# Batch 1's q and k loaded as fp32 on SyncE's queue and cast on GpSimd, in a kernel with a written-out order

## The chip, the cores and the metric

The kernel runs on one core of a Trainium2 chip. A core has TensorE (PE in the rows: matmuls, and PEld for loading weights), VectorE (DVE), ScalarE (ACT), GpSimd (POOL) and SyncE (SP), which here only issues transfers. Matmuls write PSUM; the other engines move and compute between PSUM and SBUF, GpSimd in SBUF alone. DMA engines move data between HBM and SBUF; a transfer is issued by an instruction on an engine's queue. The metric is the device time of one execution in microseconds. Each engine does its instructions in the order in which they were written, and waits for those of other engines by semaphores.

## The reference

Attention with a forget gate over 8 batches, 8 heads, 576 positions and 64 dimensions, then a bilinear feed-forward layer over its 4608 tokens:

```python
scores = scale * np.matmul(q, k.transpose(0, 1, 3, 2))
log_f = np.log(np.clip(f, 0.0001, 1.0))
cum = np.cumsum(log_f, axis=-1)
decay = cum[:, :, :, None] - cum[:, :, None, :]
scores = np.where(causal, -1000000000.0, scores + decay)
scores = scores - np.max(scores, axis=-1, keepdims=True)
attn = np.exp(scores)
attn = attn / (np.sum(attn, axis=-1, keepdims=True) + 1e-09)
attn_out = np.matmul(attn, v)
...
x = attn_out.transpose(0, 2, 1, 3).reshape(B * S, H * D)
a = x @ w_a            # 512 x 1536
b = x @ w_b            # 512 x 1536
out = a * b @ w_out    # 1536 x 512
```

Inputs and output are fp32; the kernel multiplies in fp16.

## The kernel before

**Work units.** A pair is two heads of one batch; there are 32 pairs, numbered t = 4 x batch + pair. The 576 queries of a pair are five blocks (0 to 3 of 128, 4 of 64), each against the keys up to it. For a pair the steps are: scores on TensorE (`qk_group`, line 449, tile sc, PSUM); maximum on VectorE (batch 0, line 546) or decay and maximum in one pass into the tile S (line 572, later batches); exponential on ScalarE with row sums (lines 599 and 603); reciprocal on VectorE (611 and 613); normalisation on GpSimd (line 621, into PA for blocks 0 to 2 and PB for 3 and 4); transposition of the probabilities, by DMA from SyncE (635) or on TensorE (641, batch 0 and blocks 0 to 2 of batch 1) with an eviction; product with v on TensorE (663 and 679, tile pv); eviction to xT, the feed-forward input. For batch 0 the decay is added by TensorE, from the cumulative sum in the tile crow; for batch 1 it is spread over partitions by a TensorE step (514, the "spread step") and an eviction; from batch 2 on by a DMA (525).

**Feed-forward.** Tokens go in chunks of 256, 256, 256, 384, six times 512, and 384. A chunk has 12 pairs of steps psa and psb (line 950), a copy of a by ScalarE (255), a product on VectorE (961), and then the output matmuls pso (970).

**q and k.** A batch's q, and its k, come in two halves (`load_qk`). A half is four heads; the eight batches and two tensors make 32 halves. Two forms exist. In the first, a DMA on GpSimd's queue casts to fp16 on the way (line 286), and TensorE transposes 64 x 64 blocks in four quadrants (`pe_transpose`, line 307, 36 matmuls); q's scale 1/8 is applied when the transposed tile is evicted (257 and 253). In the second, a DMA on SyncE's queue brings fp32 (291) into a buffer of the ring n32, GpSimd casts it to fp16 and scales q (257 for q, 259 for k), and TensorE transposes 128 columns at a time in two row halves (18 matmuls); the eviction then has no scale (255 and 259). The ring n32 has three buffers, which v uses too. `EARLY` names the batches of the first form, and also those with other settings (three score steps for a pair, separate parts of PA); it is batches 0 and 1.

**The order.** Every step is an `Op` with an engine (or several to choose from). `ORDER` lists the 2460 numbers of the ops in the order in which their instructions are written, which sets each engine's order; `CHOICE` has a letter for each op with a choice of engine (D VectorE, A ScalarE, P GpSimd). Dependencies of the ops themselves set nothing at run time; the semaphores follow from tiles and their buffers. At the start stand the load and logarithm of f, its cumulative sum (195 and 200), the identity (masks.py), constants and paddings on GpSimd, and 24 wake steps (78), each two matmuls on the identity, on TensorE. The weights come by casting DMAs on GpSimd's queue (424).

## Time and profile before

| what | value |
|---|---|
| time, median of 3 runs | 409.13 us (408.86 to 409.19) |
| the profiled execution | 408.86 us |
| its span | 407.1 us |
| TensorE busy | 396.3 us (97%) |
| VectorE busy | 301.6 us (74%) |
| ScalarE busy | 282.5 us (69%) |
| GpSimd busy | 262.3 us (64%) |
| granted TensorE clock, mean | 0.998 |
| DMA queue of SyncE and ScalarE (q1), share of 16 engines | 72.2% |
| DMA queue of GpSimd (q0), share of 16 engines | 11.2% |

A row of the order of time gives start, duration, engine, line, operation, tiles and shapes, a count of like instructions in a row, and in brackets the idle time before it and what ended that. A matmul's duration includes its way through the array, so two starts tell the pace, not two durations. A row of groups gives a count, busy time and mean duration in ns.

### The profile page before, as it was taken

To read this page: it belongs to the slowest core of one execution; us is meant where nothing else is said; L and a number is where in the kernel's file an instruction comes from. 1 tells how busy PE (TensorE), PEld (TensorE's weight loads), DVE (VectorE), ACT (ScalarE), POOL (GpSimd) and SP (SyncE) were. 2 spreads that over 40 slices of the span, in tenths; PEclk is the share of its full clock that TensorE was granted. 3 is DMA by queue.
4 is the path that set the end of the run, shared out by engine and by line. 5 is a ranking of instruction groups with operands and counts; after the bars stand their busy time and mean duration, and the time that the engine had idled before them with its cause. 6 is when DMAs were issued, how large, how long until landed. Compare 5 with 4: busy or idle time off the path is not lost.

```text
span 407.1 us, 11321 instructions
## 1 busy us (share of the span) xinstructions
PE 396.3 (97%) x4028; PEld 213.4 (52%) x4028; DVE 301.6 (74%) x1007; ACT 282.5 (69%) x796; POOL 262.3 (64%) x490
## 2 busy tenths in 40 slices
PE   6899999999999999999999999999999999999996
PEld 2457675766755554444445454444444444444552
DVE  3887998997979778878868789688888874442241
ACT  3898988888977778778787877568785873231230
POOL 8997697778876786886787767849666555000000
PEclk9999999999999999999999999999999999999999
DMA  8999998999999999999999999999895768100102
GB/s 126 205 190 199 152 217 194 203 271 233 249 196 221 320 229 208 276 199 229 204 275 253 278 237 166 317 250 206 205 189 159 143 116 179 52 2 32 74 0 77
DMA packets 147176, 76.65 MB, mean 188 GB/s; under 512 B 124336, under 2 KB 129200, under 8 KB 147120
## 3 DMA queue, kind: packets, MB, share of 16 engines
q1 hardware_dynamic: 141040, 68.73, 72.2%
q0 software_dynamic: 5936, 7.08, 11.2%
q8 instruction: 31, 0.51, 0.5%
q14 instruction: 25, 0.20, 0.2%
q10 hardware_dynamic: 144, 0.13, 0.1%
HBM read 52.05 MB, written 9.58 MB: 151 GB/s over the span
## 4 chain that ended last, share of the span: by engine, by line
PE 74%; DVE 3%; issue 1%; ACT 0%; DVEq 0%
PE pso L970 22%; PE psb L950 20%; PE psa L950 20%; PE sc L449 6%; PE pv L663 4%; PE psT L307 1%; DVE S L572 1%; DVE ht L961 1%; PE sc L679 1%; PE pv L679 0%; PE psP L641 0%; DVE qT L259 0%; DVE st L613 0%; DVE half L259 0%; DVE st L572 0%
## 5 line engine op out<-in xcount | busy, mean ns | idle before, releaser
L572 DVE CUSTOM_DVE_ANT_0 S<-sc,spread 64x576 f32<-64x576 f32 (+4 forms) x232 | 126.3, 562 | 16.3 <-PE sc L449 6.3
L950 PE MATMUL psb<-xT,wb 128*128 128x512 f16 (+2 forms) x528 | 115.3, 341 | 0.0
L950 PE MATMUL psa<-xT,wa 128*128 128x512 f16 (+2 forms) x528 | 115.2, 341 | 0.0
L255 ACT CAST a<-psa 128x512 f16<-128x512 f32 (+2 forms) x132 | 66.4, 503 | 56.6 <-PE psa L950 47.2
L621 POOL TENSOR_SCALAR PA<-PA,st 128x256 f16<-128x256 f16 (+2 forms) x192 | 89.1, 476 | 23.8 <-DVE st L613 19.3
L961 DVE TENSOR_TENSOR ht<-psb,a 128x512 f16<-128x512 f32 (+2 forms) x132 | 77.4, 590 | 35.7 <-PE psb L950 30.5
L970 PE MATMUL pso<-wout,ht 128*128 128x512 f16 x432 | 99.8, 380 | 0.0
L603 ACT ACTIVATE PA<-S,st 128x256 f16<-128x256 f32 (+2 forms) x168 | 84.6, 505 | 10.9 <-DVE st L572 10.6
L621 POOL TENSOR_SCALAR PB<-PB,st 128x512 f16<-128x512 f16 (+1 forms) x96 | 67.4, 709 | 33.3 <-DVE st L613 14.3
L950 PEld LDWEIGHTS <-wa 128*128 128x128 f16 x528 | 49.1, 98 | 40.5 <-issue 2.1
L950 PEld LDWEIGHTS <-wb 128*128 128x128 f16 x528 | 49.1, 98 | 40.2 <-issue 2.0
L970 PEld LDWEIGHTS <-ht 128*128 128x128 f16 x432 | 39.8, 98 | 45.2 <-issue 0.9
L603 ACT ACTIVATE PB<-S,st 128x512 f16<-128x512 f32 x56 | 40.1, 717 | 8.0 <-DVE st L572 7.8
L449 PE MATMUL sc<-kT,qT 64*128 64x128 f16 (+4 forms) x384 | 34.4, 266 | 2.4 <-ACT PA L603 0.9
L603 ACT ACTIVATION_READ_ACCUMULATOR PA<-S,st 128x1 f32 x168 | 32.1, 191 | 0.0
L259 DVE CAST xT<-pv 128x512 f16<-128x512 f32 (+1 forms) x40 | 23.1, 578 | 5.0 <-PE pv L663 4.8
L449 PEld LDWEIGHTS <-qT 64*128 64x128 f16 (+1 forms) x384 | 13.5, 95 | 23.8 <-issue 16.2
L613 DVE RECIPROCAL st<-st 128x2 f32<-128x2 f32 x128 | 18.1, 157 | 10.2 <-ACT PB L603 5.9
L599 ACT ACTIVATE PB<-S,st 128x576 f16<-128x576 f32 x28 | 21.7, 776 | 5.5 <-POOL PA L621 1.9
L259 DVE COPY osb<-pso 128x512 f32<-128x512 f32 x17 | 11.7, 688 | 17.9 <-PE pso L970 17.8
L255 ACT COPY osb<-pso 128x512 f32<-128x512 f32 x18 | 10.4, 579 | 20.6 <-PE pso L970 14.4
L663 PEld LDWEIGHTS <-nv 128*64 128x64 f16 x640 | 19.1, 109 | 10.2 <-issue 8.4
(100 smaller groups left out, 475.6 us busy)
## 6 DMA issues: line engine op xcount, KB each, us to landing
spread<-cum_d SPq DMA_DIRECT2D x24, 576.0 KB, 5.9
out_dram<-osb SPq DMA_DIRECT2D x35, 256.0 KB, 2.8
v<-in_v_dram SPq DMA_DIRECT2D x32, 256.0 KB, 5.5
q<-in_q_dram SPq DMA_DIRECT2D x12, 576.0 KB, 6.3
k<-in_k_dram SPq DMA_DIRECT2D x12, 576.0 KB, 6.4
wout<-in_moe_w_out_dram POOLq DMA_DIRECT2D x3, 512.0 KB, 9.0
v<-in_v_dram SPq DMA_DIRECT2D x8, 128.0 KB, 3.8
wa<-in_moe_w_a_dram POOLq DMA_DIRECT2D x2, 512.0 KB, 9.0
```

Of the source, the lines that this page charges most:

```text
L255: nc.scalar.copy(out=out_, in_=in_)
L259: VEC[e].tensor_copy(out=out_, in_=in_)
L449: nc.tensor.matmul(out=dst, lhsT=lhsT, rhs=rhs, start=start, stop=stop, skip_group_check=True)
L572: nc.vector.tensor_tensor_reduce(out=o, in0=x, in1=y, scale=-1.0, scalar=3e38, op0=ADD, op1=MIN, accum_out=m)
L599: nc.scalar.activation(out=p_blocks(t, 4), in_=T[("s" if direct else "z", t, 4)], func=EXP, bias=st[:, 8:9], scale=sign, accum_out=st[:, 1 ...
L603: nc.scalar.activation(out=p_blocks(t, i)[:, :, h, :], in_=(T[("s", t, i)][:, h, :] if direct else T[("z", t, i)][:, h * n:h * n + n]).rea ...
L613: nc.vector.reciprocal(out=st[:, 20 + 2 * i:22 + 2 * i], in_=st[:, 10 + 2 * i:12 + 2 * i])
L621: VEC[e].tensor_scalar(out=p, in0=p, scalar1=st[:, c:c + 1], scalar2=1.0, op0=MUL, op1=MUL)
L663: nc.tensor.matmul(out=o[HP[h], 128 * i:128 * i + 128], lhsT=vt[:, j, pr + NP * h, :], rhs=pt[:, base_blk[i] + 2 * block_at(t, i, j) + h, ...
L950: nc.tensor.matmul(out=p[:, 0:n], lhsT=w16[:, db, 128 * fb:128 * fb + 128], rhs=xTflat[db][:, t0:t0 + n], start=(db == 0), stop=(db == 3))
L961: nc.vector.tensor_tensor(out=ht[:, 0:n], in0=T.pop(("psb", t0, fb))[:, 0:n], in1=T.pop(("a16", t0, fb))[:, 0:n], op=MUL)
L970: nc.tensor.matmul(out=o, lhsT=T[("ht", t0, fb)][:, 128 * tb:128 * tb + 128], rhs=wout16[:, fb, :], start=(fb == 0), stop=(fb == 11))
```

## The change

A new tuple `CASTD` (batch 0 only) takes the place of `EARLY` where the form of q's and k's loading is chosen. Batch 1's four halves change from the first form to the second: four casting DMAs on GpSimd's queue go, four DMAs on SyncE's queue and four casts on GpSimd come, the four transposing steps have 18 matmuls instead of 36, and q's scale moves from the eviction to the cast. The ops become 2464. `ORDER` and `CHOICE` are made anew for all engines; 103 ops have a choice in both.

```diff
-        if b in EARLY:
+        if b in CASTD:
             if b == 0 and half:
...
-        x = x if b in EARLY else x.rearrange("p t h d -> p t (h d)")
+        x = x if b in CASTD else x.rearrange("p t h d -> p t (h d)")
...
-            for j in range(2 if b in EARLY else 1):
+            for j in range(2 if b in CASTD else 1):
...
-             T.pop(("psT", which, b, pr))[:, 0:S].rearrange("p (t g) -> p g t", t=TG), b in EARLY and which == "q")
+             T.pop(("psT", which, b, pr))[:, 0:S].rearrange("p (t g) -> p g t", t=TG), b in CASTD and which == "q")
...
     EARLY = tuple(range(2))
+    CASTD = tuple(range(1))
...
-            if b in EARLY:
+            if b in CASTD:
                 ld = Op("POOL", 0.65, lambda _, which=which, half=half: load_qk(b, which, half), gt, prio=p,
...
-            mm = Op("PE", 0.6 if b in EARLY else 0.27, ... [*cas, o_i if b in EARLY else o_c],
-                    prio=p, mode="quad" if b in EARLY else "row", name=f"pt{b}{which}{half}")
+            mm = Op("PE", 0.6 if b in CASTD else 0.27, ... [*cas, o_i if b in CASTD else o_c],
+                    prio=p, mode="quad" if b in CASTD else "row", name=f"pt{b}{which}{half}")
...
     CHOICE = """
-        DPPPAAAADDDAPAAADADDDAAADDDDDDDDAAAAADDDAAADDDAADADDDAAAAAADAAAAAAAAADAADAAAAADAAAAAAAAAADAADDADADAA DAA
+        PDPDAAAADDADPAPDADADDDADDDADDDADAAAAADAADDADADDAADDDAAAAAADADAAAAADAADAAAADAADAAADADADDADDADDAADADAAD DAD
```

By engine, with the op numbers turned into names, the new order up to the first feed-forward steps is as follows (before and after; w is a wake step, pt a transposing step of q or k, bm a spread step, ptr a transposition of probabilities, ld0v and ld1q loads of v and q, ldc the casting loads, ca the casts, ldw weights, flo a part of the cumulative sum, pe an eviction of q or k, bc an eviction of the spread step or its memset):

```
GpSimd before: ldc0k0 ident ldc0q0 ldc0k1 ldc0q1 ldwa const ldwb flo1 pads flo0 flo1 bc04 norm0.1 norm0.0
  ldc1k0 ldc1q0 ldwa*2 bc05 norm0.1 norm0.0 norm1.1 norm1.0 norm1.1 norm1.0 norm0.2 ca0v0 norm0.2 norm2.0 ldwb
  bc06 norm2.0 norm2.1*2 ldwb norm3.0 norm3.1 norm3.0 norm3.1 ldc1q1 ldwa norm0.3 norm0.4 ldc1k1 norm0.3 ldwb ...
GpSimd after:  ldc0k0 ldc0q0 ldc0k1 ldc0q1 ident const pads flo0 bc04 flo0 ca0v0 ca0v4 norm0.1 bc05 ldwb ldwa
  norm0.1 norm0.0*2 norm1.1*2 norm1.0*2 ldwa ldwb ldwa norm0.2 norm2.0 norm2.1 norm2.0 norm2.1 bc06 ca1k0 norm0.2
  norm3.0*2 norm3.1*2 ca1q0 norm2.2 norm3.2 ca1q1 ldwa norm0.3 ldwb norm0.3 ldwb norm2.2 norm1.3 norm0.4 norm1.3
  norm1.2*2 ca1k1 ...
TensorE before: w*5 pt0k0 w*2 pt0q0 w qk0.0 w qk1.0 pt0k1 w*3 qk0.1 bm4 pt0q1 w qk1.1 bm4 qk2.0 ... pt1k0 pv1 bm6
  ... pt1q0 pv3 qk1.2 psa w psb psa w psb ptr0B psa psb qk2.2 ptr0B psa psb w ptr2A1 ptr1B qk4.0 qk4.1 ... pt1k1 ... pt1q1
TensorE after:  w*4 pt0k0 w*2 pt0q0 w qk0.0 bm4 qk1.0 pt0k1 bm4 w*3 qk0.1 pt0q1 w*2 qk2.0 ... bm6 pt1k0 pv2 ...
  pv3 pt1q0 qk1.2 psa psb psa w ptr0B psb psa qk2.2 ptr0B ptr2A1 ptr1B pv0 psb pt1k1 qk4.0 qk4.1 ... pt1q1
VectorE after:  ... max0.1 max0.0 max1.1 max1.0 pe0k3 pe0k2 bc4 rc0.1 max0.2 ...
SyncE before: ld0v4 ldf1 ldf0 (store of sums) ld0v0 ld0v2 ld1v4 ld1v0 ld1v2 ld2q0 ...
SyncE after:  ld0v4 ldf1 ldf0 ld0v0 ld0v2 (store of sums) ld1k0 ld1q0 ld1q1 ld1v0 ld1k1 ld1v4 ld1v2 ld2q0 ...
```

More of the change, by code (lines that the diff above doesn't have):

```diff
@@ L301, in pe_transpose @@
         x = T[("n16", which, b, half)]
-        x = x if b in EARLY else x.rearrange("p t h d -> p t (h d)")
+        x = x if b in CASTD else x.rearrange("p t h d -> p t (h d)")
         p = [ps.tile([128, 1024], FP16, tag="ff", bufs=3, name="psT") for _ in range(2)]
         for t in range(TG):
-            for j in range(2 if b in EARLY else 1):
+            for j in range(2 if b in CASTD else 1):
                 for m, r in enumerate(HP):
-                    nc.tensor.matmul(out=p[m][HP[j] if b in EARLY else slice(0, 128), 64 * t:64 * t + 64],
-                                     lhsT=x[r, j, t, :] if b in EARLY else x[r, t, :], rhs=ident16[r, r],
+                    nc.tensor.matmul(out=p[m][HP[j] if b in CASTD else slice(0, 128), 64 * t:64 * t + 64],
+                                     lhsT=x[r, j, t, :] if b in CASTD else x[r, t, :], rhs=ident16[r, r],
                                      is_transpose=True, start=(t == 0), stop=(t == TG - 1), skip_group_check=True)
@@ L388, in batch_inputs @@
                     cas.append(ca)
-            mm = Op("PE", 0.6 if b in EARLY else 0.27, lambda _, which=which, half=half: pe_transpose(b, which, half), [*cas, o_i if b in EARLY else o_c],
-                    prio=p, mode="quad" if b in EARLY else "row", name=f"pt{b}{which}{half}")
+            mm = Op("PE", 0.6 if b in CASTD else 0.27, lambda _, which=which, half=half: pe_transpose(b, which, half), [*cas, o_i if b in CASTD else o_c],
+                    prio=p, mode="quad" if b in CASTD else "row", name=f"pt{b}{which}{half}")
             nx.append(mm)
@@ L1176 @@
+        2425 2424 2427 2426 2429 2428 2431 2430 2433 2432 2435 2434 2437 2436 2439 2438 2441 2440 2443 2445 2444
+        2447 2442 2446 2448 2449 2452 2450 2453 2451 2454 2457 2455 2458-2460 2456 2462 2461 2463
     """
     CHOICE = """
-        DPPPAAAADDDAPAAADADDDAAADDDDDDDDAAAAADDDAAADDDAADADDDAAAAAADAAAAAAAAADAADAAAAADAAAAAAAAAADAADDADADAA DAA
+        PDPDAAAADDADPAPDADADDDADDDADDDADAAAAADAADDADADDAADDDAAAAAADADAAAAAADADAAAADAAADAAADADADDADDAADDADAAD DAD
     """
```

66 lines of the change are left out of this document (36 added, 30 removed), and 144 rows, old and new, of the table ORDER.

## The prediction

> **What bounds the kernel now.** I read the page's busy times first, then the busy times by stretch, then the order of time of TensorE, GpSimd and VectorE in the first 50 us, and last the groups by shape.
>
> ```profile
> span 407.1 us, 11321 instructions
> PE 396.3 (97%) x4028; PEld 213.4 (52%) x4028; DVE 301.6 (74%) x1007; ACT 282.5 (69%) x796; POOL 262.3 (64%) x490
> ```
>
> ```profile
> 0.00:33.00 33.00, 27.38 (x450) 13.62 (x450) 23.61 (x51) 24.29 (x73) 29.21 (x75) 1.00 1.02 175
> 33.00:50.00 17.00, 16.04 (x283) 12.19 (x280) 14.61 (x43) 15.75 (x43) 12.19 (x20) 1.00 1.04 176
> 50.00:344.00 294.00, 293.50 (x2972) 158.34 (x2971) 243.75 (x883) 227.00 (x653) 220.89 (x397) 1.00 0.96 220
> ```
>
> The columns are the stretch, its length, then busy time of TensorE, its weight load, VectorE, ScalarE and GpSimd, the granted clock, DMA share and GB/s. From 50 us to 344 us TensorE lacks 0.5 us in 294: there a new order can hardly win, only lose. Before 33 us it is another machine: GpSimd is busy 29.2 of 33 us and TensorE fills its gaps with dummy matmuls (the wake steps). TensorE's first feed-forward matmul starts at 33.05 us, and everything after it is a queue of TensorE work. So the change is worth what it does to the moment at which that queue is reached, what it takes out of the queue, and the waits that it puts in. Batch 1 comes in exactly there.
>
> **The change, part by part.** *TensorE's transposes.* The four transposing steps of batch 1 go from 36 matmuls in quadrants to 18 in row halves each, 72 instructions fewer.
>
> ```profile
> 7.32 0.48 PE L307 MATMUL psT<-ident,k 64*64 64x64 f16 x36
> 7.73 1.26 PE L78 MATMUL wake<-ident 128*128 128x512 f16 x4
> ...
> 62.91 0.44 PE L307 MATMUL psT<-ident,q 64*128 64x64 f16 x18
> 63.18 0.38 PE L449 MATMUL sc<-kT,qT 64*128 64x512 f16 x2
> ...
> 66.31 0.44 PE L307 MATMUL psT<-ident,q 64*128 64x64 f16 x18
> 66.68 1.04 PE L970 MATMUL pso<-wout,ht 128*128 128x512 f16 x4
> ```
>
> From start to next start 36 cost 0.41 us, ahead of a full-array matmul; 18 cost 0.27 us ahead of a matmul in the same row halves and 0.37 us ahead of a full-array one. So a change of array mode costs 0.10 us, and the transposes alone 0.31 and 0.27: four times 0.04 us, two of them ahead of 33 us where gaps hide them. I take -0.1 us for all.
>
> *Mode changes in the new order.* Sorting TensorE's steps by mode (full, row halves, column halves, quadrants) the order before has 225 changes, the new one 218. From the score step of pair 8 to the last value step both have 142. From the first score step of pair 4 to that of pair 8 it is 42 against 35: 7 x 0.10 = -0.7 us. That stretch is dense in TensorE, so this is won unless another wait takes it.
>
> *GpSimd's start.* The new order issues all four casting loads of batch 0, then builds the identity, the constants and the paddings, and only then does its part of the cumulative sum; two weight loads that stood here move behind.
>
> ```profile
> 1.33 0.92 POOL L286 DMA_DIRECT2D k<-in_k_dram  x1 [0.81 <-POOLq L1209]
> ...
> 2.78 0.73 POOL L286 DMA_DIRECT2D q<-in_q_dram  x1
> 3.52 0.71 POOL L286 DMA_DIRECT2D wout<-in_k_dram  x1
> 4.23 0.72 POOL L286 DMA_DIRECT2D wout<-in_q_dram  x1
> 4.94 0.64 POOL L424 DMA_DIRECT2D wa<-in_moe_w_a_dram  x1
> ...
> 9.82 0.61 POOL L424 DMA_DIRECT2D wb<-in_moe_w_b_dram  x1
> ...
> 10.50 1.05 POOL L200 TENSOR_TENSOR crow<-cum_f,crow 32x256 f16<-32x256 f32 x1
> 11.60 0.41 POOL L102 MEMSET qd<- 128x128 f16 x2
> ...
> 14.14 1.64 POOL L200 TENSOR_TENSOR crow<-cum_f,crow 32x320 f16<-32x320 f32 x2
> 15.84 0.21 POOL L521 MEMSET spread<- 128x128 f32 x1
> 16.13 0.83 POOL L621 TENSOR_SCALAR PA<-PA,st 128x256 f16<-128x256 f16 x2
> ...
> 22.74 1.03 POOL L259 CAST nv<-v 128x1024 f16<-128x1024 f32 x1
> ...
> 27.39 1.62 POOL L621 TENSOR_SCALAR PA<-PA,st 128x128 f16<-128x128 f16 x4
> ```
>
> Loads 0.92 + 0.73 + 0.71 + 0.72 from 1.33: 4.4 us. Identity 0.53 (from 2.25 to 2.78): 4.95, so the first wake step starts some 2 us later than before, and the first transpose (7.32) some 1 to 2 us later; v's loads are now in flight beside q and k as well. The first scores wait for 12.8 us, below, which covers both up to about 3 us. Constants 4.24 (5.58 to 9.82): 9.2. Paddings 2.54 (11.60 to 14.14): 11.75. First part of the sum 1.05: 12.8 (before 11.55). Memset of the spread tile 0.21, second part 0.82: 13.85 (before 15.8; VectorE now does the other halves). Two casts of v, at most 1.03 each: under 15.9. Then the first normalisation can be due, and it is not yet: TensorE's order puts a spread step (it needs the second part, 13.85) ahead of the scores of pair 1, which started at 12.51 and now start near 14.1.
>
> ```profile
> 12.51 0.34 PE L449 MATMUL sc<-kT,qT 64*128 64x256 f16 x4
> ```
>
> ```profile
> 12.07 1.79 DVE L546 TENSOR_REDUCE st<-sc 128x2 f32<-128x512 f32 x3 [0.35 <-PE sc L449]
> 13.78 0.75 DVE L259 COPY kT<-psT 128x576 f16<-128x576 f16 x1
> ```
>
> VectorE then has pair 1's two maxima (about 0.6 and 0.4 of the 1.79 for three), three evictions of 0.75 ahead of the reciprocal for which the first normalisation waits. The scores need about 0.7 us before the first maximum can start: 14.8 + 1.0 + 2.2 = 18.0 us against 16.13. That is +1.9 us at the start of GpSimd's packed stretch.
>
> *GpSimd's packed stretch.* Four load issues of 0.72 to 0.92 us become four casts.
>
> ```profile
> L621 POOL TENSOR_SCALAR PB<-PB,st 128x512 f16<-128x512 f16 x64 | 43.9, 691 | 28.6 <-DVE st L613 13.0 <-ACT a L255 4.7 <-DVE st L572 4.6
> ...
> L621 POOL TENSOR_SCALAR PA<-PA,st 128x384 f16<-128x384 f16 x64 | 37.0, 583 | 7.4 <-DVE st L613 7.2
> ...
> L621 POOL TENSOR_SCALAR PA<-PA,st 128x256 f16<-128x256 f16 x64 | 30.3, 476 | 8.2 <-DVE st L613 5.4 <-ACT PA L603 2.2
> ...
> L621 POOL TENSOR_SCALAR PA<-PA,st 128x128 f16<-128x128 f16 x64 | 23.5, 370 | 8.2 <-DVE st L613 6.6 <-ACT kT L255 1.0
> ...
> L259 POOL CAST k<-k 128x1152 f16<-128x1152 f32 x12 | 13.7, 1144 | 1.3 <-DMA k<-in_k_dram 1.3
> ```
>
> Before, from 16.13 to 29.0 (27.39 + 1.62), GpSimd did the 18 normalisations of the first blocks of pairs 0 to 3 (8 x 0.370 + 8 x 0.476 + 2 x 0.583 = 7.9 us), two load issues 1.5, four weight issues 2.6, two memsets 0.4 and a cast of v 1.0: 13.4 us by single durations in 12.9 us of time, a factor 0.96. The new list up to the same normalisation has the 18, five weight issues 3.2, two memsets 0.4, one cast of k 1.14: 12.7 x 0.96 = 12.2 us, so it ends at 30.2. Then up to the cast of the second half of k: two q casts 2.3 (the row of the spread, further below), five normalisations of 0.583 (2.9), five of the fourth and fifth block at 0.69 (3.5), three weight issues 1.9 and the cast itself 1.1: 11.7 x 0.96 = 11.2, ending at 41.4. This is the one place where the new casts touch TensorE: its step that transposes this half stands ahead of the first scores of pair 4.
>
> *The landmark.* That score step starts here:
>
> ```profile
> 41.08 0.34 PE L449 MATMUL sc<-kT,qT 64*128 64x256 f16 x4 [0.21 <-ACT PB L603]
> ...
> 49.03 0.61 PE L950 MATMUL psa<-xT,wa 128*128 128x256 f16 x4
> 49.48 0.60 PE L950 MATMUL psb<-xT,wb 128*128 128x256 f16 x4
> ```
>
> In the new order it cannot start before 41.4 + 0.27 = 41.7: +0.6 us. By then TensorE has done two feed-forward steps fewer (0.45 us each from start to start, for 4 x 256 columns), one value step more (7 x 128 columns, 0.4 us at the same rate) and the k transpose more (0.3): +0.2 us still to do. The wake steps are all done in both.
>
> *SyncE's queue.* It gets four issues more, and they wait for the three fp32 buffers: each load of batch 1 waits for the cast that frees its buffer.
>
> ```profile
> L291 SPq DMA_DIRECT2D k<-in_k_dram x12: 367/396/4006, 59.7 to 267.4; - x12
> ```
>
> ```profile
> k<-in_k_dram SPq DMA_DIRECT2D x12, 576.0 KB, 6.4
> ```
>
> An issue costs SyncE 0.4 us, a load 6.4 us to landing. The second half of k waits for the first q's cast (done near 31.3), lands near 38, and its cast's turn comes at 40.3: covered by 2 us. Behind these waits in SyncE's order stand v of batch 1 and the loads of batch 2, no store and no transpose yet. v of batch 0 is issued ahead of the store of the cumulative sums, for which only the spread loads of the later batches wait. The weights' second halves are issued about 33 to 36 us, and TensorE wants the first of them some 2.5 us after the landmark; before, it had them earlier. I cost that at nothing, with up to 1 us if their landing is late.
>
> *Evictions.* Eight steps net go from ScalarE to VectorE, which has 50 us of 294 free in the middle stretch; nothing, and at most an eviction's 0.75 us where one stands ahead of a score's release.
>
> **The sum** against the profiled execution (span 407.1, 408.86 us with what lies around it): +0.6 + 0.2 - 0.1 - 0.7 = 0.0, so 408.86. The median of the runs is 0.27 us above that execution, so I say 409.1 us: no change that can be told. The ends: the landmark between -1.3 us (GpSimd starts its stretch at 16.13 after all and its cast ends 1.9 us sooner) and +3.4 (0.6 and 2.8 us of waits in GpSimd's list); mode changes between -0.7 and 0; later waits between -0.5 and +1.
>
> **One rule against the change.** All fp32 casts of the trace, and VectorE's copies of the same stages:
>
> ```profile
> L257 POOL TENSOR_SCALAR q<-q x12: 1140/1150/1155, 59.8 to 283.2; 128x1152 f16<-128x1152 f32 x12
> ```
>
> ```profile
> L259 DVE COPY kT<-psT x8: 737/749/757, 13.8 to 298.7; 128x576 f16<-128x576 f16 x8
> ```
>
> If GpSimd's casts and VectorE's instructions shut each other out, four more casts could take up to 4 x 1.15 = 4.6 us of VectorE's time in a stretch where it is 86% busy; with half of that on the path the time would be 411.4. Twelve casts spread over 225 us lie within 15 ns, eight copies within 20 ns, while both engines were busy most of the time: hardly. By the Trainium skill, page SBUF — State Buffer, section Who interferes with whom, a VectorE instruction in a two-port mode or with two inputs in SBUF and a GpSimd instruction contend for one port pair, and the later one waits for the whole of the other. By that rule a delay would show as a second, longer duration; this trace shows none in these rows, and they say nothing of VectorE's other forms.
>
> **The rivals.** *Slower: the cast of k's second half comes late.* Place: GpSimd's list up to 41.4, the transpose behind it, pair 4's first scores behind that, all in fixed order. The profile speaks for it: before, the same kind of list stopped once between 39.8 and 44.4.
>
> ```profile
> 44.44 0.69 POOL L621 TENSOR_SCALAR PB<-PB,st 128x512 f16<-128x512 f16 x1 [4.60 <-PE sc L449]
> ```
>
> There nothing stood behind it on TensorE; now a cast does. My 0.96 allows no wait at all in 23 us. It decides when the cast ends later than 42.3 (0.9 us late passes the bound of 0.2%); with 2.8 us of waits, somewhat over half of that one row, the time is 411.9. Against it: the list is ordered so that the oldest normalisations come first.
>
> *Faster: the start isn't late.* If the evictions ahead of the first reciprocal fit into gaps, GpSimd's stretch starts at 16.13, the cast ends 1.9 us sooner and the landmark comes at 39.8 instead of 41.7: 407.2. For it: GpSimd's list itself is 0.7 us shorter by single durations. Against it: VectorE was 23.6 of 33 us busy, and its order is fixed.
>
> *No effect at all* is inside the forecast: both ways of loading are hidden from 50 us on.
>
> **How the numbers follow.** Forecast 0.42, within 407.6 to 410.4 (faster 0.09, within 0.2% 0.24, slower 0.09: the bound is 0.8 us, about what a measurement of this kernel can tell from no change). Late cast 0.30, slower. Early start 0.22, faster but for 0.01. Port pair 0.06 (0.04 slower, 0.02 no change). So faster 0.30, same 0.27, slower 0.43; the time is the forecast's, the likeliest case. The range runs from 407.0 (early start) to 412.9 (late cast with another 1.0 us of waits): it leaves out less than 2 in 10.
>
> **What would show it.** In the new profile: first wake step near 5.0 us and first normalisation near 18.0; the last normalisation of pair 3's first two blocks ending near 30.2; the cast of k's second half ending near 41.4 and pair 4's scores following within 0.4 us; 648 transposing matmuls; TensorE's middle stretch again within 1 us of full. Wrong it would be made by a start of GpSimd's stretch off by over 1 us, by TensorE waiting for a cast or a weight, or by waits between 50 and 344 us that the order before didn't have.

## The result, and the profile after

The changed kernel takes 413.39 us (median, 412.02 to 416.55) where the kernel before took 409.16 us on the same chip: a ratio of 1.0113, 95% interval 1.0091 to 1.0135. It is slower, by 4.2 us. The profiled execution took 412.37 us, 3.5 us more than that of before. So 0.7 of the 4.2 us are in no trace. The times also scatter more: 4.5 us between the fastest and the slowest, 1.0 us before.

The page of the changed kernel, its busy times:

```profile
span 410.6 us, 11181 instructions
PE 396.3 (97%) x3956; PEld 213.1 (52%) x3956; DVE 306.9 (75%) x1015; ACT 278.5 (68%) x788; POOL 264.3 (64%) x490
```

TensorE is as busy as before (396.3 us) and the span is 3.5 us longer: all of it is time in which TensorE does nothing. Busy times by stretch (columns as in the prediction), of the changed kernel and then of the one before for the last stretch:

```profile
0.00:33.00 33.00, 26.50 (x376) 12.77 (x377) 22.56 (x48) 23.00 (x68) 28.27 (x73) 1.00 1.00 196
...
50.00:344.00 294.00, 291.58 (x2958) 157.87 (x2956) 249.89 (x894) 225.13 (x651) 220.50 (x396) 1.00 0.95 217
...
150.00:190.00 40.00, 38.29 (x356) 18.48 (x354) 31.14 (x109) 29.09 (x81) 28.56 (x51) 1.00 1.03 235
```

```profile
150.00:190.00 40.00, 39.95 (x366) 19.24 (x365) 32.46 (x118) 32.14 (x88) 29.98 (x56) 1.00 0.97 220
```

The stretch from 50 to 344 us, which lacked 0.5 us, now lacks 2.4, and 1.7 of that lies in the 40 us from 150 to 190. A second measure holds from here on: the **lag**, by how much later TensorE starts a step than it started the same step in the profile of before. In the changed kernel it is 2.42 us at pair 4's first scores, but 0.50 at the sixth psa step; 0.76 at the second feed-forward chunk (71 us), 0.72 at the fifth (150 us), 2.65 at the sixth (192 us) and 3.22 at the last psa step. Up to the fifth and the sixth chunk both orders have done the same steps, so these lags are lost time; ahead of that a lag also depends on which steps have been put off. So some 0.8 us are lost at the start, 1.9 us between 150 and 192 us, 0.6 us later.

What stopped TensorE in the middle, in the order of time of the changed kernel, TensorE and then GpSimd:

```profile
170.32 0.34 PE L450 MATMUL sc<-kT,qT 64*128 64x128 f16 x4 [0.57 <-DVE st L573]
171.24 0.44 PE L307 MATMUL psT<-ident,q 64*128 64x64 f16 x18 [0.58 <-POOL q L257]
```

```profile
163.31 0.87 POOL L532 TENSOR_SCALAR_AFFINE_SELECT spread<-spread 128x768 f32<-128x768 f32 x1 [1.71 <-DMA spread<-cum_d]
...
168.17 0.41 POOL L539 TENSOR_SCALAR_AFFINE_SELECT spread<-spread 128x256 f32<-128x256 f32 x1
...
170.03 1.16 POOL L257 TENSOR_SCALAR q<-q 128x1152 f16<-128x1152 f32 x1
```

Read from below: TensorE waits for a cast of q (batch 4) at 170.03 and, through VectorE, for the mask of pair 15's last block at 168.17 (the rows with TENSOR_SCALAR_AFFINE_SELECT: GpSimd masks a pair's decay once the load has spread it). Both stand behind the mask of pair 16 (163.31), which waited 1.71 us for its spread load. SyncE's order says why that load was late; the changed kernel first, then the one before:

```profile
147.07 0.39 SPq L526 DMA_DIRECT2D spread<-cum_d  x1
148.85 2.10 SPq L636 DMA_TRANSPOSE PTB<-PB  x1
151.05 3.71 SPq L636 DMA_TRANSPOSE PTA<-PA  x1
154.81 1.20 SPq L266 DMA_DIRECT2D v<-in_v_dram  x2
156.11 0.95 SPq L526 DMA_DIRECT2D spread<-cum_d  x1
```

```profile
155.09 0.44 SPq L525 DMA_DIRECT2D spread<-cum_d  x1
```

```profile
162.98 0.86 POOL L531 TENSOR_SCALAR_AFFINE_SELECT spread<-spread 128x768 f32<-128x768 f32 x1
```

The new order issues pair 16's load 1.0 us later than the one before (156.11 against 155.09), behind two transposes that hold SyncE 5.8 us and two loads of v; the mask can start 7.2 us after the issue. GpSimd's turn for the mask comes only 5.5 us after the issue (163.31 - 1.71 - 156.11), where the mask ran 7.9 us after it before (162.98 - 155.09). So GpSimd finds nothing yet, and everything behind the mask in its fixed order is late.

### The profile page after: what moved, and what is told of

Same layout as the page of the kernel before. It is cut to its first block, busy times and chain, and to the rows that moved or that the text cites. A ratio compares the mean times of both kernels' runs of the same rounds, so it can differ in the third digit from the quotient of the medians.

```text
span 410.6 us, 11181 instructions
## 1 busy us (share of the span) xinstructions
PE 396.3 (97%) x3956; PEld 213.1 (52%) x3956; DVE 306.9 (75%) x1015; ACT 278.5 (68%) x788; POOL 264.3 (64%) x490
## 4 chain that ended last, share of the span: by engine, by line
PE 52%; DMA 2%; ACT 1%; DVE 1%; POOL 1%; issue 1%; SPq 0%; DVEq 0%
PE psb L951 15%; PE psa L951 15%; PE pso L971 14%; PE sc L450 3%; PE pv L664 2%; DMA out_dram<-osb 2%; PE psT L307 1%; ACT PA L604 1%; DVE S L573 1%; POOL PA L622 1%; PE sc L680 0%; ACT PB L604 0%; POOL q L257 0%; DVE osb L259 0%; PE pv L680 0%
## 5 line engine op out<-in xcount | busy, mean ns | idle before, releaser
L622 POOL TENSOR_SCALAR PA<-PA,st 128x384 f16<-128x384 f16 (+2 forms) x192 | 90.0, 480 | 22.1 <-DVE st L614 17.0
L532 POOL TENSOR_SCALAR_AFFINE_SELECT spread<-spread 128x768 f32<-128x768 f32 x24 | 20.9, 870 | 6.4 <-DMA spread<-cum_d 6.3
```

The lines of the kernel that those rows point to most:

```text
L532: nc.gpsimd.affine_select(out=c[:, :, 0:SM].rearrange("p h (j k) -> p h j k", k=128), in_=c[:, :, SM:2 * SM].rearrange("p h (j k) -> p h j ...
L622: VEC[e].tensor_scalar(out=p, in0=p, scalar1=st[:, c:c + 1], scalar2=1.0, op0=MUL, op1=MUL)
```

## The experiments

Each kernel is an edit of the order alone, but where the form is named. The ratio is to the kernel before on the same chip. The last column is the lag in the profiled execution at the second, fifth and sixth chunk and at the last psa step.

| run | median us (range, n) | ratio, 95% interval | lag: 2nd, 5th, 6th, last |
|---|---|---|---|
| the changed kernel | 413.39 (412.02 to 416.55, 4) | 1.0113 (1.0091 to 1.0135) | 0.76, 0.72, 2.65, 3.22 |
| new_again | 413.07 (412.02 to 413.41, 4) | 1.0093 (1.0075 to 1.0111) | 1.40, 1.35, 3.33, 3.76 |
| new_then_old_c2 | 410.67 (410.08 to 411.81, 6) | 1.0043 (1.0028 to 1.0057) | 1.61, 1.47, 1.47, 2.43 |
| new_then_old_c5 | 412.03 (410.45 to 412.50, 4) | 1.0069 (1.0045 to 1.0093) | 2.31, 2.27, 2.78, 2.66 |
| old_in_150_190 | 411.40 (410.65 to 412.92, 4) | 1.0054 (1.0034 to 1.0075) | 2.70, 2.67, 3.19, 3.76 |
| new_form_old_order | 409.97 (409.27 to 414.86, 10) | 1.0046 (1.0018 to 1.0073) | 0.84, 0.82, 0.82, 0.71 |
| new_order_old_form | 414.62 (412.41 to 415.39, 6) | 1.0125 (1.0101 to 1.0150) | 1.85, 2.28, 2.71, 4.10 |
| old_then_new_c2 | 412.78 (411.51 to 414.96, 6) | 1.0088 (1.0060 to 1.0117) | 0.72, 1.23, 2.15, 2.67 |
| spread16_early | 411.27 (410.94 to 412.18, 6) | 1.0052 (1.0032 to 1.0072) | 0.96, 0.93, 1.21, 2.01 |
| spread16_stores | 411.62 (410.88 to 412.47, 6) | 1.0055 (1.0036 to 1.0074) | 1.36, 1.59, 2.27, 2.75 |
| casts_moved | 412.76 (410.55 to 414.98, 6) | 1.0086 (1.0056 to 1.0115) | 1.29, 1.82, 4.97, 5.86 |
| stores_early | 413.89 (411.80 to 417.31, 6) | 1.0121 (1.0087 to 1.0154) | 0.77, 1.34, 4.83, 5.24 |
| stores_casts | 412.74 (411.01 to 414.60, 6) | 1.0090 (1.0059 to 1.0122) | 1.71, 1.68, 2.28, 2.69 |
| wake_in_gap | 412.77 (412.51 to 413.21, 4) | 1.0093 (1.0075 to 1.0112) | 0.77, 0.74, 1.62, 3.39 |
| ident_first | 413.84 (411.12 to 415.16, 4) | 1.0104 (1.0069 to 1.0139) | 1.74, 1.69, 2.86, 3.77 |
| spread_behind_pair1 | 413.88 (412.56 to 415.11, 4) | 1.0113 (1.0088 to 1.0139) | 1.53, 1.24, 3.58, 4.90 |
| start_mended | 411.96 (410.18 to 413.31, 6) | 1.0068 (1.0046 to 1.0089) | 2.19, 2.14, 2.46, 3.62 |
| old_start_mended | 412.42 (411.96 to 413.77, 6) | 1.0082 (1.0061 to 1.0102) | 1.25, 1.44, 2.44, 3.18 |
| mended_then_old_c5 | 413.13 (411.51 to 415.80, 6) | 1.0105 (1.0073 to 1.0137) | 0.66, 0.63, 2.51, 4.11 |

**The form or the order?** The new form of batch 1 in the old order, and the old form in the new order:

```diff
 GpSimd (order before), new_form_old_order:
-  norm0.0 ldc1k0 ldc1q0 ldwa      norm3.1 ldc1q1 ldwa      norm0.4 ldc1k1 norm0.3
+  norm0.0 ca0v4 ldwa   norm2.0 ca1k0 ldwb   norm3.1 ca1q0 ldwa   norm0.4 norm0.3   norm1.4 ca1k1 ca1q1
 GpSimd (new order), new_order_old_form:
-  norm2.1 bc06 ca1k0    norm3.1 ca1q0    norm3.2 ca1q1 ldwa    norm1.2 ca1k1 ca1v0
+  ca0v4 ldc1k0 ldc1q0 norm0.1 ... norm3.2 ldc1k1 ldc1q1 ldwa   norm1.2 ca1v0
```

> The new form for batch 1 in the order before: the four casting loads leave GpSimd's list, four loads on SyncE's and four casts on GpSimd's come in at the nearest places that the three fp32 buffers allow (two casts of v of batch 0 move up for it); all else stands as before. By A the form costs next to nothing: 408.7 to 409.9 us, the lag at the second chunk within 0.8 us. By rival B, by which the form is what costs, the lag is there at pair 4's first scores (over 1 us) and at the end: 410.5 us or more.

> The new order with batch 1 in the old form: casting loads on GpSimd's queue, its four casts left out, TensorE's transposes 36 matmuls, the four loads gone from SyncE's queue; the order of all else is the new one. If the order is what costs (A and C) it is as slow as the changed kernel within 1 us: 411.5 to 413.5 us, with the same waits at 170 us. By B it comes back to 409 to 410 us.

The form alone measured 409.97 us, 1.1 us more than the kernel before on its chip (408.84) and clear of noise: a hair above the 409.9 of theory A, below the 410.5 of rival B. The order alone, with the old form, is as slow as the changed kernel or slower; but its trace has no wait of TensorE at 170 us, against what was expected, and its lag grows by only 0.43 us between the fifth and sixth chunks. The rest of its 4.10 us comes at the start and behind the sixth chunk. The lag of the form alone is 0.8 us at the first transpose (8.12 against 7.32 us, where GpSimd's and SyncE's lists are still those of before), 0.5 at pair 1's scores and 0.83 from the sixth psa step on; then it does not grow. Its middle is that of before to a hundredth:

```profile
50.00:344.00 294.00, 293.51 (x2964) 158.60 (x2964) 244.46 (x885) 227.92 (x656) 221.71 (x399) 1.00 0.95 221
```

So batch 1's loads and casts cost nothing in the middle, and most of the loss is the order made anew; why the form in the old order takes 1.1 us more stays open.

**Which part of the order?** Prefixes of one order followed by what is left of the other:

```diff
 all engines, cut at a TensorE step (psa 12: second chunk, psa 48: fifth, psa 60: sixth):
+  new_then_old_c2: new up to psa 12, then before
+  new_then_old_c5: new up to psa 48, then before
+  old_in_150_190:  new up to psa 48, before up to psa 60, then new
+  old_then_new_c2: before (old form) up to psa 12, then new
```

> The new order of all engines up to the first matmul step of the second feed-forward chunk (33 to 71 us of it, batch 1's loads and casts included), then the order before for everything that is left. Theory A (the middle of the new order costs most: TensorE's lag on the order before is 0.76 us at that step, 0.72 us at the fifth chunk, 2.65 us at the sixth, 3.2 us at the end): the start's 0.8 us stays and the rest goes, 409.9 us, ratio 1.002. Rival B (the new form and the start's order set off a delay that only comes out later, through queues and buffers): 412 us or more. Lag at the sixth chunk 0.8 us by A, over 2 us by B.

> The new order up to the first matmul step of the fifth chunk (150 us), the order before from there. By A the lag there is 0.7 us and stays: 409.9 us. By B, or if the loss between 150 and 190 us was prepared earlier (spread loads that the new order issues 13 us later, v of batch 4 9 us later, both before 157 us), the lag at the sixth chunk is 1.5 to 2.7 us and the time 411 to 412.4 us.

> The new order with one stretch taken from the order before: from the first matmul step of the fifth chunk to that of the sixth (150 to 190 us). By A the 1.9 us lost there do not come, and the 0.7 us ahead of it and some 0.6 us behind it stay: profiled 410.4 us against 412.4 us. By B 412 us or more.

> The kernel before (old form) up to the first matmul step of the second chunk, then the new order for everything that is left: the counterpart of the first run. If start and middle cost separately, the lag at the second chunk is 0 within 0.2 us, the waits at 150 to 190 us are there as in the changed kernel, and the time is 411 to 412.3 us. If the late start is what makes the middle late (the loads and casts find their places taken), the waits in the middle go as well: 409 to 410.3 us.

The new start alone costs 1.8 us (410.67 against 408.84), more than the 0.8 us of the first profile, and between the 409.9 of theory A and the 412 of rival B: the lag at the second chunk was 0.76 to 2.70 us in traces that begin with the very same instructions. In its own trace 1.0 us of the lag comes behind the sixth chunk, where the order is the old one.

With the old middle the lag grows between the fifth and the sixth chunk by 0.5, 0.5 and 0.0 us, with the new middle by 1.9 and 2.0 (the changed kernel's two traces). The two hybrids with 0.5 began with a lag of 2.3 and 2.7 us, so that their times are higher than theory A had them; for A speaks the growth alone.

Behind the old start the new order is still at 412.78 us, so it needs no late start to lose. But it does not lose there by the same waits: pair 16's mask waited for nothing, the waits at 170 us are not there, and its growth of 0.9 us goes with others (0.36 us for a transposed tile, 0.76 us behind a copy to osb, the output's buffer). Its lag was 0.72 us at the second chunk already, not the 0 that was expected. That start and middle cost separately is so not shown.

**One late load?** A single transfer moved in SyncE's order:

```diff
 SyncE, spread16_early:
   spread15
+  spread16
   tr13B tr13A ld4v0
-  spread16
   store8
```

> The changed kernel with one transfer moved: the spread load of pair 16 comes directly behind that of pair 15 in SyncE's order (147 us) instead of behind two transposes and a load of v (156 to 158 us). In seven traces of the new middle GpSimd's mask of pair 16 waited 0.5 to 2.8 us for this load; behind it in GpSimd's order stand the mask of pair 15's last block and the q cast, for which TensorE waited at 170 to 172 us, 0.4 to 2.3 us, and where that was 2.3 us the granted clock fell to half for some 3 us behind it. By this theory (E) the wait of GpSimd and TensorE's waits at 170 to 172 us go, the lag from the fifth to the sixth chunk grows by 0.3 to 1.0 us instead of 1.9 to 3.5, and the median is 0.9 to 1.8 us below the changed kernel's 413.1 to 413.4 us. If the waits only move on to the next late transfer, it stays above 412.6 us.

411.27 us, 1.8 to 2.1 us less than the changed kernel, and a range of 1.2 us. SyncE, GpSimd and TensorE of this kernel, and its stretch from 150 to 190 us:

```profile
147.24 0.98 SPq L526 DMA_DIRECT2D spread<-cum_d  x2
```

```profile
155.53 0.41 POOL L539 TENSOR_SCALAR_AFFINE_SELECT spread<-spread 128x256 f32<-128x256 f32 x1 [4.29 <-DVE st L573]
...
161.80 0.87 POOL L532 TENSOR_SCALAR_AFFINE_SELECT spread<-spread 128x768 f32<-128x768 f32 x1
...
166.85 0.41 POOL L539 TENSOR_SCALAR_AFFINE_SELECT spread<-spread 128x256 f32<-128x256 f32 x1
...
168.70 1.16 POOL L257 TENSOR_SCALAR q<-q 128x1152 f16<-128x1152 f32 x1
```

```profile
169.93 0.34 PE L450 MATMUL sc<-kT,qT 64*128 64x128 f16 x4
170.22 0.44 PE L307 MATMUL psT<-ident,q 64*128 64x64 f16 x18
```

```profile
150.00:190.00 40.00, 39.63 (x365) 18.98 (x364) 32.79 (x114) 30.37 (x86) 29.91 (x54) 1.00 1.05 242
```

The mask of pair 16 waits for nothing, what stands behind it runs 1.3 us earlier, and both waits of TensorE are gone: it lacks 0.37 us instead of 1.71. A wait of GpSimd of 4.29 us stays in this trace (4.24 in the changed kernel's) and costs nothing: nothing that TensorE needs soon stands behind it. With the wait of 1.71 us went 1.64 us of the lag's growth (1.92 to 0.28). The kernel is still 2.3 us above the one before.

Traces of other kernels bear it out. With the load where the new order has it, the mask waited 0.46 (new_order_old_form), 0.88 (wake_in_gap), 1.01 (ident_first), 1.16 (new_again), 1.41 (spread_behind_pair1), 1.71 (the first trace) and 2.80 us (stores_early), and the lag grew by 0.43, 0.88, 1.17, 1.97, 2.35, 1.92 and 3.48 us. With the load moved, in four kernels, the mask waited for nothing and the lag grew by 0.28 to 1.00 us. Of the two kernels with casts moved forward, stores_casts fits (0.73 and 0.60 us) and casts_moved does not (0.78 and 3.15 us, by waits elsewhere).

**Other moves in the middle.** Two casts of batch 4 forward on GpSimd; two output stores forward on SyncE; both; the stores with the spread load (mask16 is the mask of pair 16, mask14last that of pair 14's last block):

```diff
 GpSimd, casts_moved (and stores_casts):
   ca4k1
+  ca4q1
   mask14last mask15 ... norm14.1
+  ca4v0
   mask16 qd16
-  ca4v0
   norm14.3 ... norm15.2
-  ca4q1
 SyncE, stores_early (and stores_casts, spread16_stores):
   tr12B
+  store6
   tr12A ld4q1
-  store6
   spread15
+  store7
   tr13B ... spread18
-  store7
```

> The changed kernel with two casts moved forward on GpSimd: batch 4's second q half into the wait of 4.24 us ahead of the mask of pair 14's last block (151 to 155.3 us), and batch 4's first v ahead of the mask of pair 16, which waited 1.71 us for its spread load. By A the two waits of TensorE at 170.3 us (0.57 us, scores behind VectorE, which waited for GpSimd's mask) and 171.2 us (0.58 us, the q cast) go, the lag from the fifth to the sixth chunk grows by 0.5 to 0.9 us instead of 1.93, and the median falls by 0.9 to 1.2 us. By a rival, by which TensorE only meets the next wait a little later (the output store at 180 us), it falls by less than 0.4 us.

> The changed kernel with two output stores moved forward in SyncE's order: store 6 ahead of the transpose of pair 12's first blocks (its copy ends at 142.5 us, the order issues it at 146.6), and store 7 behind the spread load of pair 15 (its copy ends at 146.9 us, the order issues it at 179.9, 33 us later; the order before waited 7.4 us). Theory D (with two output buffers a store that is issued late or lands late holds up a copy of pso, that holds a PSUM buffer, and TensorE waits: 0.24 us at 188 us in the first trace, 0.24 and 0.44 us at 153 and 188 us in the second, 1.28 us at 231 us in a third) expects no wait of TensorE for a copy to osb between 150 and 190 us, the 0.6 us wait for the q cast at 171 us still there, and a median 0.3 to 0.8 us below the changed kernel's. If the stores are no cause, the median stays within 0.3 us.

> The two stores moved forward, and the two casts of the earlier run (batch 4's second q half and first v) as well. With the casts moved alone, TensorE waited 0.5 us for a transposed tile at 149 us and 0.8, 0.6 and 0.65 us behind copies to osb at 154, 184 and 190 us, in place of the 1.15 us that had gone. By A and D together nothing but the 0.28 us at 156 us is left: the lag grows by 0.4 to 0.8 us between the fifth and sixth chunks instead of 1.93, and the median is 1.0 to 1.8 us below the changed kernel's, at 411.3 to 412.1 us. If the waits only move on again, it stays above 412.5 us.

> The spread load of pair 16 and the two output stores moved forward together. By D and E no wait of TensorE over 0.3 us is left between 150 and 190 us, the lag grows by 0.2 to 0.7 us there, and the median is 411.2 to 412.2 us. If earlier transfers only crowd each other out, it stays above 412.6 us.

With the casts moved the wait for q went, as expected, but in its profiled execution others came, for copies to osb among them, and the median fell by only 0.3 to 0.6 us. The stores alone took away the waits behind copies to osb and gave no time (413.89 us), so as a cause they fall. Both together kept the lag's growth to 0.60 us, but the median of 412.74 us missed the 411.3 to 412.1 expected. The stores with the spread load are no better than the spread load alone; TensorE then waited 0.58 us for a transposed tile at 161 us. The trace of stores_early shows how the late load can cost much more than its delay; GpSimd, TensorE, and stretches:

```profile
164.57 0.87 POOL L532 TENSOR_SCALAR_AFFINE_SELECT spread<-spread 128x768 f32<-128x768 f32 x1 [2.80 <-DMA spread<-cum_d]
```

```profile
171.58 0.34 PE L450 MATMUL sc<-kT,qT 64*128 64x128 f16 x4 [1.74 <-DVE st L573]
...
172.50 0.66 PE L307 MATMUL psT<-ident,q 64*128 64x64 f16 x18 [0.58 <-POOL q L257]
```

```profile
170.00:175.00 5.00, 2.84 (x54) 2.19 (x54) 3.65 (x14) 3.63 (x10) 4.96 (x8) 0.72 0.98 226
175.00:180.00 5.00, 5.00 (x25) 2.29 (x24) 4.01 (x11) 2.99 (x8) 1.72 (x3) 0.94 1.21 229
```

This time the load made GpSimd wait 2.80 us and TensorE 2.3; the granted clock then fell (0.72 and 0.94 over these two stretches of 5 us), and the lag jumped by 3.4 us within three psa steps (1.36 to 4.76).

**The start.** The changed kernel, run again:

> The changed kernel once more, nothing edited: a second trace of it, beside the three below. Two traces of kernels that begin with the same 150 us as it show TensorE's granted clock at 0.50 from 15 to 18.4 us, where TensorE had been busy 0.27 to 0.42 of the two microseconds before 14; the first trace of the changed kernel shows 1.00 there. Theory C (the new start leaves a hole between TensorE's first steps that now and then costs it half its clock for 3.4 us) expects times that scatter over 2 us or more here and a lag at the second chunk of either 0.8 to 1.6 us (clock 1.00) or 2.3 to 2.7 us (clock 0.50). Theory A expects the waits of 170 to 171 us again, 1.1 us together.

Its clock stayed at 1.00, its lag at the second chunk was 1.40 us, and it waited for the q cast again (0.57 us), but not for the scores; its times scatter over 1.4 us, not 2. The mean granted clock of a run tells whether the clock fell: it is 0.994 to 0.996 in the five traces with a fall ahead of their last 5 us, 0.998 to 1.000 in the others. All eight runs of the changed kernel, that of 416.55 us too, have 0.998 to 1.000. So neither its loss nor its scatter comes from the clock. But a fall is there at the start of two of the hybrids. TensorE's busy share and clock by microsecond in new_then_old_c5 (clock: third column from the end):

```profile
11.00:12.00 1.00, 0.69 (x20) 0.15 (x8) 0.97 (x2) 0.99 (x2) 0.92 (x2) 1.00 1.23 263
12.00:13.00 1.00, 0.27 (x6) 0.26 (x8) 0.93 (x3) 1.00 (x3) 0.94 (x2) 1.00 1.31 264
13.00:14.00 1.00, 0.35 (x16) 0.32 (x11) 0.97 (x2) 0.76 (x2) 0.92 (x2) 1.00 1.22 202
...
15.00:16.00 1.00, 1.00 (x43) 0.69 (x38) 0.89 (x2) 1.00 (x6) 1.00 (x2) 0.50 0.45 119
...
18.00:19.00 1.00, 0.94 (x7) 0.24 (x7) 0.22 (x2) 0.36 (x3) 0.64 (x3) 0.81 1.04 406
```

TensorE was busy 1.3 of 3 us, and ran at half its clock from 15.0 to 18.4 us. By the Trainium skill, page TensorE: Matmul & The Clock Gate, section Part 1: The HAM clock gate, the clock is halved behind an idle window of about 3.4 us and released behind a busy one. The trace agrees in the value (0.50) and in the length (3.4 us), but not in what sets it off: here a stretch of 3 us with TensorE at 44%, in stores_early 2.3 us of waits in 2.7 us, came ahead of it. Nor does such a stretch always do it: new_again's TensorE was emptier in the same place, and its clock stayed at 1.00:

```profile
12.00:13.00 1.00, 0.09 (x2) 0.09 (x4) 0.98 (x1) 0.99 (x4) 0.51 (x2) 1.00 1.28 283
13.00:14.00 1.00, 0.53 (x16) 0.41 (x16) 0.92 (x3) 0.94 (x2) 0.51 (x1) 1.00 1.16 201
14.00:15.00 1.00, 0.44 (x5) 0.20 (x7) 0.92 (x2) 0.03 (x1) 0.93 (x2) 1.00 1.28 244
```

What decides it stays open. These edits tried to mend the start:

```diff
 TensorE, wake_in_gap (and start_mended):   qk0.0 +w7 +w8 bm4 qk1.0 pt0k1 bm4 -w7 -w8 w9
 GpSimd, ident_first (and start_mended):    ldc0k0 +ident ldc0q0 ldc0k1 ldc0q1 -ident const
 TensorE, spread_behind_pair1:              qk0.0 -bm4 qk1.0 pt0k1 +bm4 bm4 w7
 ScalarE, start_mended:                     pe0k0 -table_exp pe0q0 pe0k1 pe0q1 +table_exp bc4
 VectorE, start_mended:                     max1.0 +rc0.1 pe0k3 pe0k2 bc4 -rc0.1
 SyncE, start_mended:                       spread16 as in spread16_early
```

> The changed kernel with two of its 24 wake steps moved in TensorE's order: wake 7 and wake 8 from behind the second spread step of pair 4 to between the first scores of pair 0 and that pair's first spread step, where TensorE waited from about 13.2 to 14.0 us. By C the clock is 1.00 throughout the start, the lag at the second chunk 0.8 to 1.6 us, and the median 0.3 to 1.0 us below the changed kernel's with less scatter. If the clock is no cause, the median stays within 0.3 us of the changed kernel's.

> The changed kernel with the identity built behind the first casting load on GpSimd, as in the order before, instead of behind the fourth. The prediction's step says that the later start of the wake steps (4.99 us instead of 2.89) costs nothing, since the first scores wait for GpSimd's part of the cumulative sum at 12.6 us: then pair 4's first scores stay where they are within 0.7 us and the median within 0.3 us, while a hole of over 2 us opens ahead of the first scores, and the granted clock may fall behind it. The rival, by which the start's lag comes from the late wake steps, expects the lag at the second chunk to fall by 1 to 2 us.

> The changed kernel with one spread step of pair 4 moved back behind the scores of pair 1 and a transpose in TensorE's order, as before the change. The prediction's step says that this spread step (it waits for GpSimd's second part of the sum, until 13.9 us) holds pair 1's scores back by 1.7 us and so the start of GpSimd's packed stretch by 1.9: then pair 1's scores start near 13.0 instead of 14.2 us, the first normalisation 0.5 to 1.2 us earlier than 18.2, and the lag at the second chunk falls by 0.4 to 1.0 us. The rival (GpSimd's list is filled by what comes later anyway, or the hole ahead of it costs clock) expects no change of that lag beyond 0.3 us.

> The changed kernel with the spread load of pair 16 moved forward (as in spread16_early) and its start put back at four places: the identity behind the first casting load on GpSimd; ScalarE's table load for the exponential (1.28 us, ahead of q's first evictions in the new order) behind these evictions, as before; on VectorE the first reciprocal ahead of two evictions of k and one of the spread step; and wake 7 and 8 in the hole ahead of the first spread step. If these places are the start's loss, q's first eviction runs near 9.8 to 10.9 us instead of 12.0, the first scores near 11 to 12 instead of 12.65, the first normalisation near 16.2 instead of 18.2, the granted clock stays 1.00, the lag at the second chunk is 0 to 0.5 us instead of 0.8 to 1.6, and the median 409.9 to 410.8 us. If GpSimd's part of the sum or TensorE's own work holds the start, the lag stays above 0.8 us and the median at 411.0 to 411.6 us.

None brought the lag at the second chunk down as expected. The wakes in the gap kept the clock at 1.00, but the plain kernel (new_again) had it at 1.00 as well, and the median is only 0.3 to 0.6 us lower. The identity first brought the first scores to 11.6 us, opened a hole, and the clock fell to 0.50 from 14 to 17 us. With pair 4's spread step out of the way pair 1's scores began at 13.96 us instead of 14.24 (expected: near 13.0), held by ScalarE's eviction of q, and the first normalisation at 18.03 instead of 18.16:

```profile
13.96 0.34 PE L450 MATMUL sc<-kT,qT 64*128 64x256 f16 x4 [0.46 <-ACT qT L253]
```

ScalarE's order of the changed kernel shows a table load ahead of the first q eviction:

```profile
10.56 1.28 ACT L188 ACT_TABLE_LOAD   x1
...
11.96 0.63 ACT L253 ACTIVATE qT<-psT 128x576 f16<-128x576 f16 x1
```

With that moved too, the first scores came at 11.09 us, and stopped at the next thing, GpSimd's part of the cumulative sum:

```profile
11.09 0.34 PE L450 MATMUL sc<-kT,qT 64*128 64x256 f16 x4 [0.22 <-ACT qT L253]
13.60 0.34 PE L450 MATMUL sc<-crow,pick 64*128 64x256 f16 x4 [2.16 <-POOL crow L200]
```

The clock fell behind that hole as well (0.50 from 15.2 to 18.6 us). So identity, table load and GpSimd's list each hold the start at about the same time; taking one away shows the next, and a hole can cost the clock. A second trace that begins with the same instructions (mended_then_old_c5, below) had its first scores at 10.67 us, its first normalisation at 16.37 us, about as before the change, and the clock at 1.00. Its lag at the second chunk was 0.66 us all the same, so an early first normalisation alone does not bring the lag down.

**Both causes away.**

```diff
+  old_start_mended:   new_form_old_order up to psa 12, then new with spread16, store6 and store7 forward
+  mended_then_old_c5: start_mended (spread16 not moved) up to psa 48, then before
```

> The new form in the order before up to the second chunk, and from there the new order with the spread load and the two stores moved forward: both causes taken away, the form and the rest of the new order kept. If start and middle are the whole of the loss, 409.6 to 410.8 us, 0.3 to 1.0 us above the new form in the order before. If the new order loses elsewhere, 411.5 us or more.

> The same mended start and the new order up to the first matmul step of the fifth chunk, the order before from there: nothing of the new middle. If start and middle are all that the change loses, this is within 0.8 us of the kernel before, 408.3 to 409.8 us; it is the candidate for a version faster than both. If it stays above 410.2 us, the new order loses elsewhere ahead of the fifth chunk.

Both missed, at 412.42 and 413.13 us. In the first, TensorE waited 0.72 us for a k cast just behind the cut (75.7 us) and then for a transposed tile; in the second for transposed tiles too, in an order that had no such wait when it ran from the start. Its lag grew by 1.9 us between the fifth and sixth chunks, with nothing of the new middle. The longest waits:

```profile
161.31 0.36 PE L664 MATMUL pv<-PTA,nv 128*64 128x128 f16 x6 [1.24 <-DMA PTA<-PA]
```

```profile
183.72 0.25 PE L664 MATMUL pv<-PTB,nv 128*64 128x128 f16 x2 [1.14 <-DMA PTB<-PB]
```

Why transposes land late in these hybrids stays open, and with it some 2 us of the loss; no version faster than the kernel before was found.

## Why the prediction was wrong

I said 409.1 us, between 407.0 and 412.9; it is 413.39.

*Right: the walk through the start.* First wake step 4.99 us (said near 5.0), pair 1's scores 14.24 (14.1), first normalisation 18.16 (18.0), 648 transposing matmuls, and the last normalisation of pair 3's first two blocks at 28.12 + 2.19 = 30.31 us (30.2). GpSimd's rows:

```profile
18.16 0.48 POOL L622 TENSOR_SCALAR PA<-PA,st 128x256 f16<-128x256 f16 x1 [2.51 <-DVE st L614]
...
28.12 2.19 POOL L622 TENSOR_SCALAR PA<-PA,st 128x384 f16<-128x384 f16 x5
...
38.88 2.08 POOL L622 TENSOR_SCALAR PB<-PB,st 128x512 f16<-128x512 f16 x3 [1.31 <-DVE st L614]
40.93 1.16 POOL L622 TENSOR_SCALAR PA<-PA,st 128x384 f16<-128x384 f16 x2
42.02 1.16 POOL L259 CAST k<-k 128x1152 f16<-128x1152 f32 x1
```

The reason that I gave for pair 1's scores, the spread step, was only the last of several.

*Mis-sized: the landmark.* The cast of k's second half ended at 43.18 us, not 41.4: 1.31 us of it is the wait that my factor 0.96 left out and that the rival of the late cast put there. Pair 4's scores came 2.42 us late, not 0.6:

```profile
43.23 0.44 PE L307 MATMUL psT<-ident,k 64*128 64x64 f16 x18 [0.53 <-POOL k L259]
43.51 0.33 PE L450 MATMUL sc<-kT,qT 64*128 64x256 f16 x4
```

But at the sixth psa step the lag was 0.50. Between these two steps TensorE had the same amount to do in both kernels, not 0.2 us more in the changed one: about 4.7 us of columns at the pace of its full-array matmuls (0.86 us for four of 512 columns), if a matmul on half or a quarter of the array counts as that share. The kernel before took 7.95 us for it, with waits of 0.27 and 0.28 us for ScalarE, the changed one 6.02 us. So the rival's place was right, its price of 2.8 us was not paid, and that the sum came out near its 0.0 at this step is in part luck: the landmark was 1.8 us later than forecast, and 1.3 us more than forecast was caught up behind it.

*Fits, but not shown alone: the mode changes.* I took 0.7 us off for seven changes. By the traces the changed kernel has 6 in that stretch, the one before 12, and from there to the second chunk both have 22. So the gain can be part of what was caught up; no run has it alone.

*Right in part: the form.* I priced the new form itself at -0.1 us. SyncE's four issues, the casts and the transposes add no lag in the middle of new_form_old_order; that kernel is 1.1 us slower than the one before even so, and no run shows by what. Casts and VectorE's copies do not hold each other up, against the port-pair rival: the rows have one duration still, now with two more q casts and two more copies.

```profile
L257 POOL TENSOR_SCALAR q<-q x14: 1141/1152/1160, 30.3 to 288.0; 128x1152 f16<-128x1152 f32 x14
```

```profile
L259 DVE COPY kT<-psT x10: 747/754/758, 15.8 to 311.3; 128x576 f16<-128x576 f16 x10
```

*The step that failed: "later waits between -0.5 and +1".* I had written that from 50 to 344 us a new order can hardly win, only lose, and then walked the first 50 us in detail and gave the other 294 a margin of one sentence. From the second chunk to the last psa step they cost 2.5 us (lag 0.76 to 3.22), 1.9 of them between the fifth and sixth chunks. The step named no wait there; the first trace showed two, 0.57 and 0.58 us, both behind one spread load that two transposes and a load of v had been put ahead of. With that load alone moved forward 1.6 of the 1.9 us went, and the median fell by 1.8 to 2.1 us, into the range. This could be read in the two orders: for each mask on GpSimd, where its load stands on SyncE and what stands behind the mask. What made the 0.6 us behind the sixth chunk, and the 0.8 us of the start where the sum had 0.0, stays open.

*Left out, and no part of this miss: the clock.* I took the granted clock as 1.00 and let holes ahead of 33 us cost their length. In the changed kernel that held. Of ten traces that begin with its instructions two had half the clock for 3.4 us behind such a hole; their lag at the second chunk is 2.31 and 2.70 us, that of the other eight 0.76 to 1.71.

## What to carry to other kernels

In a kernel with fixed orders, a wait is priced by what stands behind the waiting instruction: a wait of 4.3 us on GpSimd was free, one of 1.7 us cost TensorE about as much, and moving one transfer forward gave it back. When an order is made anew, compare for every transfer its distance from issue to first use in both orders over the whole run, and not only where the edit lies. A gain or loss of one part says little about the sum: hybrids of two orders got waits that the profiles of neither whole order show in that place.

## What the runs showed that was not expected

The clock can fall without a long gap: TensorE at 44% over 3 us, with no single gap over 1.05 us, or 2.3 us of waits within 2.7, was followed by 0.50 for 3.4 us; 35% over 3 us in another trace was not. Traces of the same first instructions differ by up to 1.9 us at the second chunk (0.76 to 2.70 us of lag), part of it by this. In the stretch from 120 to 200 us a spread load took 4.9 to 7.1 us from issue to landing in the changed kernel, 4.8 to 8.1 before, where the trace has the landing. A mask whose turn came 5.5 or 5.6 us behind the issue missed it in both traces of the changed kernel; with 13.6 to 14.1 us it was met in all four kernels with the load moved.
